# Traced durations in a planner's costs for the tails' norms, and the second chunk's front behind the first chunk's work

## The chip, the cores and the metric

The kernel runs on one core of one Trainium2 chip. The metric is the device time of one execution in microseconds. The engines and queues have short names: PE is the TensorE matmul engine (PEld its weight loads), DVE is VectorE, ACT is ScalarE, POOL is GpSimd, SP is the queue that issues most DMAs. "Filler" below means work that PE has in its queue between two steps of one chain.

## The reference

A transformer block with modulation from a condition vector, over 2048 rows of 512 columns. A is attention with 32 heads of 16 columns, B a mixer with shifted columns and an MLP of 1792 columns.

```
h = _layernorm(x) * (1 + ca) + sa
x = x + ga * _A_ref(h, A_wqkv, A_wo)          # attention, then @ wo
h = _layernorm(x) * (1 + cb) + sb
x = x + gb * _B_ref(h, B_w1, B_w2, B_w3, B_w4)
# _B_ref(x):
h = gelu(layernorm(x) @ w1)                   # then each quarter of the columns is shifted by rows: +1, -1, +2, -2
x1 = x + hs @ w2
return x1 + gelu(layernorm(x1) @ w3) @ w4
```

So each row goes through `wo`, a norm with its own scale and shift (the front's first norm), a second norm, `w1`, a gelu, the shift, `w2`, a third norm, `w3`, a gelu and `w4`.

## The kernel before

The 2048 rows are four chunks of 512 rows, and a chunk is four tiles of 128 rows (tiles 0 to 3 are chunk 0, 4 to 7 chunk 1, and so on). All matrices are split into a high and a low part, so that each product is three matmuls (L360, L362, L364). Attention takes the first 1510 us of the profiled execution; what comes behind it is called the tail here and runs to the end.

The tail of a chunk is a Python generator, `tail(ci)`, and behind it `rest(ci)`. Its steps on PE are, in order:

- **oT**: 16 transposes of the attention's output (`osb`, L1260), which ACT (L354) and DVE (L350) split into the tile `A`.
- **wo**: 12 matmuls of 512 columns for each row tile. Behind a tile's `wo` stands its norm chain: x1_add (DVE L1425), statistics (DVE L371, L372, L1367), a power on POOL (L1370), the functions `center` (DVE L1434) and `scale` (DVE L1437), statistics again, three small POOL instructions (L1370, L1374, L1375; the function `shift`), and the application on ACT (L1381), which writes the tile `xn` (chunk 0) or `xf` (chunks 1 to 3).
- **T**: 8 transposes of `xn` or `xf` for a pair of row tiles (L1260), split again into `A`. T(1,0) is the first pair of chunk 1, T(1,1) the second.
- **w1**: matmuls of 256 columns, and a gelu of six instructions over ACT, DVE and POOL (L1475 to L1479).
- **w2**: 12 matmuls of 512 columns for a row tile, xb_add (DVE L1530), the third norm (L371 to L1381), and a scaling (DVE L1534) and an addition (POOL L1535) that the output needs.
- **T4**: transposes of the third norm's `xn`.
- **w3** and **w4** in pairs of 128 columns of the MLP (`fi` counts them): w3 with a gelu, w4 onto `x1`. In chunk 0 the weights of w3 and w4 are split afresh, from the tile `raw` into `wr`: POOL L1223 for w4, ACT L1224, DVE L1225.

The order on each engine is fixed when the program is built, by a planner (`Sched`). It keeps a clock per engine in which every step advances by a written cost. `one()` walks a list of generators from the front and lets the first one whose gate is open place its next matmul on PE; `chain` queues the steps of other engines, `misc` places them when the planned clock of their engine comes near. A norm's transposes are placed on PE when the planner believes that the norm is done: the costs decide how much other PE work stands between a `wo` and its T. On the chip every engine then works through its list in order and waits on semaphores; the plan's clock is not there any more.

Costs before, in planned ns: statistics 752, the power 464, the three POOL steps 850, ACT's application 479, `center` 1355 and `scale` 602, from the helpers

```
def cA(n=CH):
    return n / 1.2 + 52
def cD(n=CH):
    return n / 0.96 + 69
```

The generators of chunks 1 to 3 are put at the front of the list, ahead of what is left of `tail(0)`. Two gates hold chunk 1: its `tail` starts when all `w1` of chunk 0 is placed, and each of its `wo` waits for the third norm of tile 2 (`("xn4", 2) in done`, since `HOLD` is 0). `x1_loads` issues the four loads of a chunk's input tiles from ACT's queue (L1317) when its `tail` starts.

Of the kernel before, what the change touches and what calls it, by code (L numbers as in the profile page):

```python
# [14 lines left out]
AF = mybir.ActivationFunctionType  # L15
# [5 lines left out]
S, D, H, DH, F = 2048, 512, 32, 16, 1792  # L21
# [21 lines left out]
XX = 170.0  # L43
# [24 lines left out]
NB = 1  # L68
# [5 lines left out]
WSPL = 1  # L74
ZPRIO = 2
NPRIO = 1
HOLD = 0
NLOW = 1
CLOW = 1150
OUTW = 7000.0  # L80
# [238 lines left out]
# [6 lines that stand above are left out]
# [7 lines left out]
def kernel(ctx, tc, A_x, A_wqkv, A_wo, B_w1, B_w2, B_w3, B_w4, c, w_mod, out):  # L332
    nc = tc.nc
    te, act, dve, pool, dma = nc.tensor, nc.scalar, nc.vector, nc.gpsimd, nc.sync
# [35 lines left out]
    def ln_stats(st, mv, src):  # L370
        dve.bn_stats(st, src)  # L371
        dve.bn_aggr(mv, st)  # L372
# [49 lines left out]
    sch = Sched()  # L422
    done = set()
# [812 lines left out]
    def pool_of(ci):  # L1236
        return fa if ci < NB or (ci - NB) % 2 else tp
# [28 lines left out]
    def spawn(gen, key):  # L1266

        def run():
            yield from gen
            done.add(key)  # L1270
        sch.add(run(), 0)
# [25 lines left out]
    def tail(ci):  # L1297
        end = ci == NC - 1
        t0 = ci * TPC
        early = ci < NB  # L1300
        if ci:
            yield lambda: ("w1", ci - 1) in done
        yield lambda: ("att", ci) in done
        new = list(range(t0, t0 + TPC))
# [40 lines left out]
        def wo_mm(i, ks):  # L1345
            if i not in banks:
                banks[i] = dbank("wo")
            A, c = As[i // 2], slice(i % 2 * P, i % 2 * P + P)
            return rows_mm(banks[i], lambda k, p: A[:, k, p, c], wo, ks, KT)
# [9 lines left out]
        def ln_ops(src, mean=False):  # L1359

            st = fa.tile([P, 6], F32, name="tst", tag="tst", bufs=8)
            mv = fa.tile([P, 2], F32, name="tmv", tag="tmv", bufs=10)
            rs = fa.tile([P, 2], F32, name="trs", tag="trs", bufs=10)

            def stats():
                ln_stats(st, mv, src)
                dve.tensor_scalar(mv[:, 1:2], mv[:, 1:2], EPS, None, op0=OP.add)  # L1367

            def rstd():
                pool.tensor_tensor(rs[:, 0:1], mv[:, 1:2], mhalf[:, 0:1], op=OP.pow)  # L1370

            def shift():
                rstd()
                pool.tensor_tensor(rs[:, 1:2], mv[:, 0:1], rs[:, 0:1], op=OP.mult)  # L1374
                pool.tensor_scalar(rs[:, 1:2], rs[:, 1:2], -1.0, 1.0, op0=OP.mult, op1=OP.mult)  # L1375
            if mean:
                return rs, mv, (("D", cD() + 150, stats), ("G", 464, rstd))
            return rs, (("D", cD() + 150, stats), ("G", 850, shift))

        def ln_apply(dst, src, rs):  # L1380
            return ("A", cA(), lambda: act.activation(dst, src, AF.Identity, bias=rs[:, 1:2], scale=rs[:, 0:1]))  # L1381

        def later(key, fn):
            yield lambda: key in done
# [4 lines left out]
        def normed(key, t, rs):  # L1389
            tag = xtag(key, t)  # L1390
            xlive[tag] = xlive.get(tag, 0) + 1
            if tag == "x4":
                x = tp.tile([P, D], F32, name="xn", tag=tag, bufs=XN[tag])
            else:
                x = xns[tag][:, xnum[tag] % XN[tag]]
                xnum[tag] += 1
            xn[key, t] = x
            y = xbt[t]
            return ln_apply(x, y, rs), mark((key, t))
# [6 lines left out]
        def xn_room(key, t):  # L1406
            return xlive.get(xtag(key, t), 0) < XN[xtag(key, t)]

        def norm_T(ts, key, i):

            yield lambda: all((key, t) in done for t in ts) and (key == "xn" or not ci or ("w3", ci - 1) in done)
            An[key, i] = A = tA("A4" if key == "xn4" else "A", i, len(ts) * P)
            yield from transposed(lambda k, j: xn[key, ts[j]][:, k * P:(k + 1) * P], range(KT), len(ts), A)
            xlive[xtag(key, ts[0])] -= len(ts)

        for i, t in enumerate(new):
            yield lambda: ci != 1 or i < HOLD or ("xn4", 2) in done
            yield lambda: sch.room() and xn_room("xn", t) and t in x1t and sch.now() >= arr.get(("x1", t), 0.0) and (ci < 2 or ("z", t - 2 * TPC) in done)
            yield from wo_mm(i, range(KT))
            b = banks.pop(i)  # L1420
            x1 = x1t[t]
            xb = xbt[t] = xbs[:, t % XBF] if pool_of(ci) is fa else tp.tile([P, D], F32, name="xb", tag="xb", bufs=XBT)

            def x1_add(x1=x1, b=b):
                dve.tensor_tensor(x1, x1, b, op=OP.add)  # L1425
                sch.free(b)

            r, m, ops = ln_ops(x1, True)
            r2, ops2 = ln_ops(xb)

            def center(xb=xb, x1=x1, m=m, ops=ops):
                ops[0][2]()
                sch.late = sch.put("G", 464, sch.T["D"] - cD() + XX, ops[1][2]) + XX
                dve.scalar_tensor_tensor(xb, x1, m[:, 0:1], cbrow, op0=OP.subtract, op1=OP.mult)  # L1434

            def scale(xb=xb, r=r):
                dve.scalar_tensor_tensor(xb, xb, r[:, 0:1], sbrow, op0=OP.mult, op1=OP.add)  # L1437

            go = partial(sch.chain, ("D", cD(), x1_add), ("D", 2 * cD() + 150, center), ("D", cD(), scale), *ops2,
                         *normed("xn", t, r2), bank=b)  # L1440
            go()
            if i % 2:
                spawn(norm_T(grp[i // 2], "xn", i // 2), ("T", ci, i // 2))
# [55 lines left out]
        for gi, ts in enumerate(grp):  # L1499
            yield lambda: ("T", ci, gi) in done  # L1500
            A = An["xn", gi]
# [19 lines left out]
        for si, ts in enumerate(sub):  # L1521
            yield lambda: all(("g", ci, i, n) in done for i in range(1 + (t0 + 1 in ts)) for n in range(4))
            for t in ts:
                yield lambda: sch.room() and xn_room("xn4", t)
                b = dbank("w2")
                yield from rows_mm(b, lambda k, p: g[:, k, p, 130 + (t - t0) * P - SH[k]:][:, :P], w, range(KT), KT)
                xb, x1 = xbt[t], x1t[t]

                def xb_add(xb=xb, b=b):
                    dve.tensor_tensor(xb, xb, b, op=OP.add)  # L1530
                    sch.free(b)

                r, ops = ln_ops(xb)
                z = (("D", cD(), lambda xb=xb: dve.scalar_tensor_tensor(xb, xb, 2.0, gbrow, op0=OP.mult, op1=OP.mult)),  # L1534
                     ("G", cG(), lambda xb=xb, x1=x1: pool.tensor_tensor(x1, x1, xb, op=OP.add)), mark(("z", t)))  # L1535
                sch.chain(("D", cD(), xb_add), *ops, *normed("xn4", t, r),
                          (None, 0, lambda z=z: sch.chain(*z, prio=ZPRIO)), bank=b, prio=NPRIO)
            spawn(norm_T(ts, "xn4", si), ("T4", ci, si))
# [88 lines left out]
    for k, blk in enumerate(blocks + [[]] * (LAG + CPER)):  # L1627
# [76 lines left out]
        if blk and blk[0] <= 2 * (NS - T0S) <= blk[-1]:  # L1704
            sch.add(tail(0))
# [9 lines left out]
    with ExitStack() as ex:  # L1715
        ep = ex.enter_context(tc.tile_pool(name="ep", bufs=1, space=PSUM))
        psd["d"], psd["s"] = ep, False
        att.close()
        akx.close()
        tpx = ExitStack()  # L1720
        tp = tpx.enter_context(tc.tile_pool(name="tp", bufs=1))
        big["A"] = tp.tile([P, 4 * KT * 2 * P], F32R, name="A")
        big["g2"] = tp.tile([P, 4 * KT * 2 * P], F32R, name="g2")
        done.add("C")
        rings["f"] = Ring(FRONT * (NC - NB), [("wf", BF)] * BF)
        for ci in range(NB, NC):
            sch.add(tail(ci), ci - NB)
        while sch.busy():
            sch.step()
        tpx.close()  # L1730
# [29 lines left out]
```

## Time and profile before

| | us |
|---|---|
| median of 3 runs (lowest, highest) | 1996.83 (1995.67, 1999.66) |
| profiled execution | 1994.44 |
| its span, first to last instruction | 1992.3 |
| PE busy in the span | 1931.4 (97%) |
| DVE, POOL, ACT busy | 1655.6, 1552.9, 1518.5 |

PE is busy nearly throughout. In the tail PE's list is long and in order, so an idle stretch of PE there is time lost; the views of the section below are read for these stretches, and for what ends each. [...]

### The profile page before, as it was taken

The numbers are of one execution on the slowest core, as the hardware profiler recorded it, in microseconds if no ns is written. First come the engines' busy times: TensorE is split into PE (matmuls) and PEld (weight loads), VectorE is DVE, ScalarE is ACT, GpSimd is POOL, SyncE is SP. The second block draws the span as 40 slices with busy tenths as digits, with TensorE's granted clock in tenths as the row PEclk, the third lists the DMA queues.
The fourth block names the chain that finished last, engine by engine and source line by source line (L and its number), as shares of the span: only waits on it lengthen the run. The fifth ranks groups of instructions, "written<-read, shape, count | busy, mean of one in ns | idle before, by whom it ended". The sixth has DMA issues, their size and how long they took to land.

```text
span 1992.3 us, 41624 instructions
## 1 busy us (share of the span) xinstructions
PE 1931.4 (97%) x14456; PEld 1155.7 (58%) x14456; DVE 1655.6 (83%) x2979; ACT 1518.5 (76%) x3100; POOL 1552.9 (78%) x1473
## 2 busy tenths in 40 slices
PE   7999999999999999999999999999998999999999
PEld 5755554554444444444444444444446888888998
DVE  6398888879999999999999999999975886656443
ACT  6438987768999999999999999999985545344333
POOL 6339998888999999999999999999995564435222
PEclk9989999999999999999999999999998999999999
DMA  8777666455434444444444444464415667553541
GB/s 303 232 193 195 163 174 173 129 134 125 97 80 101 82 99 83 99 82 100 84 98 84 98 82 99 83 161 106 97 39 197 239 247 273 208 207 120 199 148 69
DMA packets 185506, 277.99 MB, mean 140 GB/s; under 512 B 117104, under 2 KB 127856, under 8 KB 169008
## 3 DMA queue, kind: packets, MB, share of 16 engines
q1 hardware_dynamic: 181792, 267.20, 49.4%
q10 hardware_dynamic: 2304, 4.20, 0.7%
q0 software_dynamic: 1200, 3.93, 0.5%
q8 instruction: 115, 1.88, 0.4%
q14 instruction: 95, 0.78, 0.1%
HBM read 211.81 MB, written 62.91 MB: 138 GB/s over the span
## 4 chain that ended last, share of the span: by engine, by line
PE 70%; DVE 15%; ACT 5%; issue 4%; POOL 3%; DMA 2%; SPq 1%; ACTq 0%; POOLq 0%; DVEq 0%
PE mb L998 17%; PE sc L1025 11%; PE pv L1099 11%; DVE mx L994 11%; PE w L364 5%; PE w L360 5%; PE w L362 5%; PE pv L1096 5%; PE ot L1126 3%; ACT pt L1021 3%; PE xT L1260 1%; POOL trs L1370 1%; POOL pt L1074 1%; DMA wr<-Ws 1%; SPq L136 1%
## 5 line engine op out<-in xcount | busy, mean ns | idle before, releaser
L994 DVE TENSOR_REDUCE mx<-mb 128x1 f32<-128x512 f32 x2048 | 1250.9, 686 | 55.7 <-PE mb L998 48.7
L1074 POOL TENSOR_SCALAR pt<-pt 128x1024 f16<-128x1024 uint16 x773 | 1017.6, 1366 | 67.3 <-ACT pt L1021 66.9
L1021 ACT ACTIVATE pt<-sc 128x512 int32<-128x512 f32 x1688 | 890.1, 623 | 89.8 <-PE mb L998 67.5
L998 PE MATMUL mb<-kst,qtl 62*128 62x512 f32 x2048 | 786.4, 463 | 17.2 <-ACT pt L1021 7.9
L1025 PE MATMUL sc<-qtl,kst 64*128 64x512 f32 x2048 | 743.9, 450 | 3.1 <-DVE mx L994 1.8
L998 PEld LDWEIGHTS mb<-kst,qtl 62*128 62x128 f32 x2048 | 361.7, 192 | 260.7 <-ACT pt L1021 136.4
L1025 PEld LDWEIGHTS sc<-qtl,kst 64*128 64x128 f32 x2048 | 336.9, 185 | 188.4 <-DVE mx L994 119.7
L1099 PE MATMUL pv<-pt,vst 128*32 128x512 f16 x3376 | 318.0, 395 | 4.6 <-ACT ac L1116 4.6
L1479 POOL TENSOR_TENSOR g<-sq,g 128x256 fp32r<-128x256 f32 (+1 forms) x124 | 96.7, 784 | 190.0 <-ACT g L1478 177.6
L1074 POOL TENSOR_SCALAR xbs<-xbs 128x1024 f16<-128x1024 uint16 x165 | 219.4, 1362 | 4.3 <-ACT xbs L1021 4.3
L1021 ACT ACTIVATE xbs<-sc 128x512 int32<-128x512 f32 x360 | 199.8, 640 | 10.8 <-PE mb L998 9.7
L1099 PEld LDWEIGHTS <-vst 128*32 128x32 bf16 x4096 | 91.2, 94 | 182.1 <-issue 163.3
L1096 PE MATMUL pv<-pt,vst 128*32 128x512 f16 (+1 forms) x1688 | 172.5, 391 | 1.4 <-POOL pt L1074 1.3
L362 PE MATMUL w<-A,wr 128*128 128x256 f32 (+1 forms) x520 | 154.1, 296 | 0.3 <-DVE A L350 0.3
L360 PE MATMUL w<-A,wr 128*128 128x256 f32 (+1 forms) x520 | 153.9, 296 | 0.0
L364 PE MATMUL w<-A,wr 128*128 128x256 f32 (+1 forms) x520 | 153.8, 296 | 0.0
L1475 ACT ACTIVATE sq<-w 128x256 f32<-128x256 f32 (+1 forms) x130 | 52.0, 400 | 127.4 <-PE w L364 117.7
L364 PE MATMUL w<-wr,g 128*128 128x512 f32 x270 | 106.4, 394 | 3.1 <-POOL g L1479 3.1
L360 PE MATMUL w<-wr,g 128*128 128x512 f32 x270 | 106.7, 395 | 1.6 <-DMA wr<-Ws 1.6
L362 PE MATMUL w<-wr,g 128*128 128x512 f32 x270 | 106.2, 393 | 0.0
L1457 DVE SCALAR_TENSOR_TENSOR sq<-sq,w 128x256 f32<-128x256 f32 (+1 forms) x130 | 58.1, 449 | 55.4 <-ACT sq L1477 55.3
L362 PEld LDWEIGHTS w<-A,wr 128*128 128x128 f32 x520 | 99.3, 191 | 1.6 <-DVE A L350 0.5
(172 smaller groups left out, 2453.7 us busy)
## 6 DMA issues: line engine op xcount, KB each, us to landing
wr<-Ws SPq DMA_DIRECT2D x66, 1024.0 KB, 5.6
vst<-Vs SPq DMA_DIRECT2D x64, 768.0 KB, 5.1
kst<-Ks SPq DMA_DIRECT2D x126, 384.0 KB, 6.0
Ws<-wr SPq DMA_DIRECT2D x14, 1024.0 KB, 5.0
qtl<-Qs SPq DMA_DIRECT2D x128, 96.0 KB, 4.1
Vs<-vt SPq DMA_DIRECT2D x32, 384.0 KB, 4.4
Ks<-qk SPq DMA_DIRECT2D x16, 512.0 KB, 4.0
Qs<-qk SPq DMA_DIRECT2D x16, 512.0 KB, 3.0
```

Of the source, the lines that this page charges most:

```text
L360: te.matmul(o, lh, rh, start=first, stop=False)
L362: te.matmul(o, lh, rl, start=False, stop=False)
L364: te.matmul(o, ll, rh, start=False, stop=last)
L994: end = sch.crit("D", 605, e + PX, lambda: dve.reduce_max(mxs[u][:, j, g, c:c + 1], b, axis=AX.X))
L998: return ready, lambda: te.matmul(b, lhs, kst[u % 3][r, c * CH:(c + 1) * CH], start=True, stop=True), after
L1021: ea = sch.crit("A", 480, e + PX, lambda: act.activation(pt[s][:, j], b, AF.Exp))
L1025: return ready, lambda: te.matmul(b, kst[u % 3][r, kt * P:(kt + 1) * P], qst[u][r], start=True, stop=True), after
L1074: e_low[s] = XP["G"] + sch.crit("G", 1345, ready, lambda: pool.tensor_scalar(o, i, 0.5, 1.0, op0=OP.mult, op1=OP.mult))
L1096: te.matmul(acc[r:r + n, :], v[:, kt + i, c:c + n].bitcast(F16), pt[s + i].bitcast(F16)[:, j, 0::2], start=False, stop=kt == NKT - 2, skip ...
L1099: te.matmul(acc[r:r + 32, :], v[:, kt, r:r + 32], pt[s].bitcast(F16)[:, j, 1::2], start=kt == 0, stop=False, skip_group_check=True)
L1126: te.matmul(b[:, t * n:(t + 1) * n], ac[:, t * P:(t + 1) * P], smat.rearrange("p j d -> p (j d)"), start=True, stop=True)
L1479: ("G", cG(n), lambda: pool.tensor_tensor(lo, sq, hi, op=OP.subtract)), (None, 0, end), bank=b)
```

## The change

```
-HOLD = 0
...
-        if ci:
+        if ci > 1:
             yield lambda: ("w1", ci - 1) in done
...
             if mean:
-                return rs, mv, (("D", cD() + 150, stats), ("G", 464, rstd))
-            return rs, (("D", cD() + 150, stats), ("G", 850, shift))
+                return rs, mv, (("D", 1050, stats), ("G", 560, rstd))
+            return rs, (("D", 1050, stats), ("G", 1120, shift))
...
-            return ("A", cA(), lambda: act.activation(dst, src, AF.Identity, bias=rs[:, 1:2], scale=rs[:, 0:1]))
+            return ("A", 815, lambda: act.activation(dst, src, AF.Identity, bias=rs[:, 1:2], scale=rs[:, 0:1]))
...
-            yield lambda: ci != 1 or i < HOLD or ("xn4", 2) in done
...
-                sch.late = sch.put("G", 464, sch.T["D"] - cD() + XX, ops[1][2]) + XX
+                sch.late = sch.put("G", 950, sch.T["D"] - 750 + XX, ops[1][2]) + XX
...
-            go = partial(sch.chain, ("D", cD(), x1_add), ("D", 2 * cD() + 150, center), ("D", cD(), scale), *ops2,
+            go = partial(sch.chain, ("D", cD(), x1_add), ("D", 1050 + 750, center), ("D", 750, scale), *ops2,
...
         for ci in range(NB, NC):
-            sch.add(tail(ci), ci - NB)
+            sch.add(tail(ci))
```

The planner counts longer norms, `tail(1)` to `tail(3)` stand behind what is left of `tail(0)` in the list, and chunk 1 has neither of its gates. No instruction's work is changed, but 2 of the attention's last halvings of `pt` go from POOL (L1074) to ACT (L157).

The order is told at three places. Line numbers of the changed file are one to two lower there.

PE, at the end of attention, before: `xn` are the norms of tiles 2 and 3, `w1_...` the first `w1` of that pair, `osb1` chunk 1's attention output.

```order
L1260 MATMUL xT_24573<-ident_64,xn_7635 128x128 x4
L1260 MATMUL xT_24600<-ident_64,xn_7635 128x128 x4
L360 MATMUL w1_24610<-A_7633,wr_21841 128x256
...
L1260 MATMUL xT_24692<-ident_64,osb1_7627 128x128 x4
L1260 MATMUL xT_24701<-ident_64,osb1_7627 128x128 x4
L1260 MATMUL xT_24714<-ident_64,osb1_7627 128x128 x4
L1260 MATMUL xT_24719<-ident_64,osb1_7627 128x128 x4
L360 MATMUL w2_24726<-wr_24449,g1_24451 128x512
```

The same place now:

```order
L1259 MATMUL xT_24600<-ident_64,osb1_7627 128x128 x4
L1259 MATMUL xT_24606<-ident_64,osb1_7627 128x128 x4
L1259 MATMUL xT_24618<-ident_64,osb1_7627 128x128
L1259 MATMUL xT_24620<-ident_64,xn_7635 128x128 x4
L1259 MATMUL xT_24625<-ident_64,xn_7635 128x128 x4
L1259 MATMUL xT_24618<-ident_64,osb1_7627 128x128 x3
L1259 MATMUL xT_24637<-ident_64,osb1_7627 128x128 x4
L359 MATMUL w1_24646<-A_7633,wr_21841 128x256
```

All 16 oT transposes of chunk 1 now stand ahead of chunk 0's second `w1` pair, 9 of them ahead of that pair's own transposes; behind that `w1` come 15 `wo` matmuls of tiles 4 and 5, then w2 (36), then 21 more `wo` (tiles 5 and 6), and T4 behind them, with w3 right behind T4. Before, T4 followed w2 directly and 36 `wo` followed T4.

ACT at the same place, before:

```order
L1475 ACTIVATE sq<-w_24536 128x256
L1477 ACTIVATE sq<-sq 128x256
L1475 ACTIVATE sq<-w_24551 128x256
L354 ACTIVATE A<-xT 128x2x256
L1477 ACTIVATE sq<-sq 128x256
L1478 ACTIVATE g_24451<-sq 128x256
L354 ACTIVATE A<-xT 128x2x256
```

And now:

```order
L1473 ACTIVATE sq<-w_24549 128x256
L1476 ACTIVATE g_24451<-sq 128x256
L1475 ACTIVATE sq<-sq 128x256
L1316 DMA x_24592<-in_A_x_dram 128x512
L1316 DMA x_24594<-in_A_x_dram 128x512
L1316 DMA x_24596<-in_A_x_dram 128x512
L1316 DMA x_24598<-in_A_x_dram 128x512
L353 ACTIVATE A<-xT 128x2x256
L1476 ACTIVATE g_24451<-sq 128x256
L353 ACTIVATE A<-xT 128x2x256
L1380 ACTIVATE xn<-xbs,trs 128x512
L353 ACTIVATE A<-xT 128x2x256 x4
```

Tile 3's application (L1380) stood ahead of these rows before, and now stands behind the four DMA issues and two copies of `A`.

DVE between the last w2 of chunk 0 and T4's split, before (`xbs` rows are third norms, the last L1530 is tile 2's):

```order
L1530 TENSOR_TENSOR xbs<-xbs,w_24770 128x512
L371 BN_STATS tst<-xbs 128x6
L372 BN_AGGR tmv<-tst 128x2
L1367 TENSOR_SCALAR tmv<-tmv 128x1
L1534 SCALAR_TENSOR_TENSOR xbs<-xbs,gbrow 128x512
L1225 TENSOR_TENSOR wr<-raw,wr 128x512 x4
L1534 SCALAR_TENSOR_TENSOR xbs<-xbs,gbrow 128x512
L350 TENSOR_TENSOR A<-xT,A 128x384 x4
```

And now:

```order
L1528 TENSOR_TENSOR xbs<-xbs,w_24800 128x512
L1224 TENSOR_TENSOR wr<-raw,wr 128x512
L1532 SCALAR_TENSOR_TENSOR xbs<-xbs,gbrow 128x512
L1224 TENSOR_TENSOR wr<-raw,wr 128x512 x3
L370 BN_STATS tst<-xbs 128x6
L371 BN_AGGR tmv<-tst 128x2
L1366 TENSOR_SCALAR tmv<-tmv 128x1
L1423 TENSOR_TENSOR x_24594<-x_24594,wo 128x512
```

Tile 2's statistics now stand behind four splits of fresh weights and one L1532; between them and T4's first split (L349) come two x1_add, two L1532, one more split and `center` of tile 5.

## Rows read from the trace of the kernel before

**Rows 1.** Stretches: start:end, length, busy PE, PEld, DVE, ACT, POOL, PEclk, DMA, GB/s.

```profile
1510.60:1523.62 13.02, 10.52 (x74) 9.90 (x73) 5.41 (x12) 5.89 (x15) 3.54 (x6) 0.87 0.66 246
1523.62:1549.51 25.89, 21.07 (x88) 16.91 (x87) 20.63 (x40) 10.48 (x20) 11.35 (x16) 0.87 0.61 212
1549.51:1582.00 32.49, 28.92 (x172) 26.68 (x171) 29.14 (x57) 19.55 (x41) 22.59 (x30) 1.00 0.60 215
1660.00:1992.30 332.30, 323.33 (x1951) 290.65 (x1949) 175.70 (x365) 134.49 (x327) 118.91 (x178) 1.00 0.45 164
```

**Rows 2.** Waits of PE from 1500 us on: waiter, releaser, total us, times, longest.

```profile
PE xT L1260 <- ACT xf L1381: 8.6, 6, 2.0
PE xT L1260 <- ACT xn L1381: 4.8, 3, 2.9
PE w L364 <- POOL g L1479: 3.1, 2, 2.2
PE xT L1260 <- DVE sq L1457: 2.2, 1, 2.2
```

**Rows 3.** PE in order of time: start, us, instruction, [idle before, releaser].

```profile
1510.60 0.60 PE L1260 MATMUL xT<-ident,xn 128*128 128x128 f32 x4
1513.36 0.66 PE L1260 MATMUL xT<-ident,xn 128*128 128x128 f32 x4 [2.16 <-DVE sq L1457]
1516.20 0.41 PE L362 MATMUL w<-A,wr 128*128 128x256 f32 x1
1516.42 0.41 PE L364 MATMUL w<-A,wr 128*128 128x256 f32 x1
1519.20 0.28 PE L362 MATMUL w<-A,wr 128*128 128x256 f32 x1
1519.32 0.28 PE L364 MATMUL w<-A,wr 128*128 128x256 f32 x1
1523.62 0.48 PE L360 MATMUL w<-wr,g 128*128 128x512 f32 x1
1531.90 0.39 PE L364 MATMUL w<-wr,g 128*128 128x512 f32 x1
1537.77 2.40 PE L1260 MATMUL xT<-ident,xn 128*128 128x128 f32 x10 [2.94 <-ACT xn L1381]
1549.51 0.33 PE L360 MATMUL w<-A,wr 128*128 128x384 f32 x1
1554.01 0.34 PE L364 MATMUL w<-A,wr 128*128 128x384 f32 x1
1555.98 0.98 PE L1260 MATMUL xT<-ident,xf 128*128 128x128 f32 x7 [1.52 <-ACT xf L1381]
```

**Rows 4.** ACT (ACTq: its DMA issues) and DVE near the end of attention.

```profile
1511.67 0.59 ACT L354 ACTIVATE A<-xT 128x512 fp32r<-128x512 f32 x1
1512.64 0.40 ACT L1478 ACTIVATE g<-sq 128x256 fp32r<-128x256 f32 x1
1521.94 2.39 ACTq L1317 DMA_DIRECT2D x<-in_A_x_dram  x4
1512.90 0.41 DVE L1457 SCALAR_TENSOR_TENSOR sq<-sq,w 128x256 f32<-128x256 f32 x1
```

**Rows 5.** DVE, POOL and ACT between the last w2 of chunk 0 and T4.

```profile
1533.19 0.68 DVE L1530 TENSOR_TENSOR xbs<-xbs,w 128x512 f32<-128x512 f32 x1
1535.52 3.58 DVE L1225 TENSOR_TENSOR wr<-raw,wr 128x512 fp32r<-128x512 f32 x4
1535.09 0.93 POOL L1370 TENSOR_TENSOR trs<-tmv,mhalf 128x1 f32<-128x1 f32 x1 [0.26 <-DVE tmv L1367]
1536.90 0.81 ACT L1381 ACTIVATE xn<-xbs,trs 128x512 f32<-128x512 f32 x1 [0.38 <-POOL trs L1375]
```

**Rows 6.** POOL in order of time, in front of a w4 of chunk 0.

```profile
1623.54 0.99 POOL L1370 TENSOR_TENSOR trs<-tmv,mhalf 128x1 f32<-128x1 f32 x1 [6.38 <-DVE tmv L1367]
1624.50 1.01 POOL L1479 TENSOR_TENSOR g<-sq,g 128x384 fp32r<-128x384 f32 x1
```

**Rows 7.** PE in order of time, at the end of attention.

```profile
1496.89 0.40 PE L1096 MATMUL pv<-pt,vst 128*32 128x512 f16 x3 [0.72 <-POOL pt L1074]
```

## The prediction, made before the changed kernel was run

> **What bounds the kernel now.** I read the stretches of the tail first, then PE's waits, then PE in order of time at each wait, then the engine that ended it. In the tail PE is the bound: from 1660 us on it is busy 323.3 of 332.3 us [rows 1]. No matmul is added or taken away, so the change is worth what it does to PE's idle time and to the TensorE clock. From 1500 us on four kinds of wait make up 18.7 us [rows 2]: 8.6 for `xf`, six times (the second norm of chunks 1 to 3 was not done when PE came to its transposes); 4.8 for `xn` (nearly all at T4, 1532.6 to 1537.8); 3.1 for POOL's `g`; 2.2 for a bank at the end of attention. Two of the stretches also run at a mean clock of 0.87 [rows 1]. In the first, `w1` starts every 0.22 us instead of 0.12 for 16 matmuls [rows 3]: 1.6 us. In the second, ten transposes take 2.40 us where seven take 0.98 at full clock [rows 3], about 1.0 us more, and about six `wo` behind them cost some 0.2 more each: 2.2 us.
>
> **Waits for `xf`: taken away.** A norm's transposes stand where the planner thinks it done, so longer costs put more PE work between a `wo` and its T. I counted the matmuls between the second tile's last `wo` and T in both orders. They go at 0.12 us (256 columns), 0.17 (384: 1549.51 to 1554.01 is 26 starts) and 0.24 (512: 1523.62 to 1531.90 is 35) [rows 3]. The distances before and now are: T(1,0) 7.5 and 11.8; T(1,1) 13 and 19; T(2,0) 14 and 22; T(2,1) 10 and 17; T(3,0) 7.5 and 14; T(3,1) 7 and 16 us. Each grows by 4 to 9 us, and the longest wait was 2.0 [rows 2]. I take five as gone; T(1,0) I leave at its 1.52, because DVE comes to its norm late (below). That is 8.6 - 1.5 = **-7.1 us** (bounds -8.6 and -4). What hides these norms now is w1, w3 and w4 of other chunks.
>
> **The end of attention: dearer.** Before, four transposes at 1510.60 ran in a free bank, and PE then waited until 1513.36 for the bank that DVE's gelu step at 1512.90 released [rows 3, 4]. Now the first `osb` transposes are in that bank (the order names both `xT_24600`): PE waits 2.76 us instead of 2.16. Nine transposes later, at about 1514.3, it needs tile 3's `xn`. On ACT that now stands behind four DMA issues, two copies of `A` and a `g`. The issues took 2.39 us together where they stood before [rows 4]; from about 1512.8 they end at 1515.2. Then 0.59 + 0.40 + 0.59 [rows 4] and 0.81 for the application [rows 5] make 1517.6 (1516.4 if the issues pass faster). Fifteen transposes (1.8 us) and 48 `w1` (5.8) bring 1525.2 at full clock. Before, the same work ended at 1523.62, with 1.6 us of slow clock in it. PE is idle for nearly 6 us here, twice 2.8 to 3, so I expect at least as much slow clock: 1.6 us as now, at most 4.8 (all 48 `w1` at 0.10 more). The result is +1.8 to +6.5; I take **+3.0**, nearer to the lower end, since 1.6 us is what the one case seen at this place cost.
>
> [...]
>
> **Around T4: even.** Before, T4 had nothing in front of it: from the end of w2 (1532.1) to its third norm (1537.77) is 5.6 us. Now 21 `wo` stand there, 5.0 us of cover. But DVE has four splits of weights ahead of tile 2's statistics, 3.58 us [rows 5], and the chain becomes 8.3 to 9.2 us; PE waits about 3.5 instead of 4.8: -1.3. What is late next is T4's split. Between these statistics and the split, DVE has four instructions of 0.68, a split of 0.9 and a `center` with its statistics (about 1.8): 5.4 us. POOL, ACT and the first transposes take 3.6 of it (from the end of the statistics at about 1535.0 to 1537.77, and a copy) [rows 3 to 5]. `wo` covered this before; w3 follows at once now, so PE waits about 2.4 (1 to 3). The slow clock of the stretch should cost some 1 us less, since part of it falls into this wait. Sum **0** (-3 to +3). Behind it DVE still has tile 6's `center` ahead of tile 5's second statistics, therefore the 1.52 at T(1,0) stays.
>
> [...]
>
> **Other terms.** A w4 waited 2.2 us for a `g` that stood on POOL behind a power, and POOL had waited 6.38 us for DVE's statistics [rows 2, 6]. With 950 for the power and 1050 for the statistics the plan puts later `g` nearer to where POOL is; I take half, **-1.1** (0 to -2.2). Chunk 0's w3 and w4 now come earlier against chunk 1's w1, on weights that DVE must have split: **+1.0** (0 to +5) for new waits. Two halvings move from POOL, for which PE waited 0.72 [rows 7], to ACT: **-0.4** (-0.7 to +0.7). The early loads cost SP nothing: they go from ACT's queue, which is counted above. The other gate (`("w1", 0)`) only lets oT forward.
>
> **Sum.** +3.0 + 0 - 7.1 - 1.1 + 1.0 - 0.4 = -4.6 us. The profiled execution, 1994.44, becomes 1989.8; it stands 2.4 under the median, so the median goes from 1996.83 to **1992.2**, or -0.23%. About 0.2% (4 us) is what a measurement of this kernel can tell from no change; the forecast lies just outside.
>
> **The rivals.**
> *The front eats it.* The clock stays low through all 48 `w1` (+3 over my term) and DVE comes late to T4's split (+1): -4.6 + 4 = -0.6, so 1996.2. For it: two stretches with idle PE and 0.87 today [rows 1]. Against it: the slow clock cost only 1.6 us there today, behind a wait of 2.16.
> *Slower: DVE becomes the bound between T(1,0) and w2 of chunk 1.* From 1549.5 to 1582 DVE is busy 29.1 of 32.5 us already [rows 1]. The change brings one more pair of w3 and w4 into that place: four splits at 0.9 [rows 5] and their gelu and additions, some 8 us of DVE against 8.4 us of PE, so DVE's 3.4 us of slack is needed for the norms that fell behind at T4. If it falls short by 4.5 us or more, PE waits that long, and norms behind it are late again (1.5 and 2.0 at T(2,0) and T(2,1) return): -4.6 + 4.5 + 3.5 + 1 = +4.4, so 2001.2. It decides where w3 waits for `wr` from DVE; before there is no such wait [rows 2].
> *The plan doesn't do what it says* would need the T's not to move; the order shows that they do.
>
> **How the numbers follow.** The forecast has 0.5, with its own range 1987 to 1994; the front eating it 0.33; slower 0.17. About a tenth is left out on each side. 1987.0 is where the waits for `xf` and `g` go wholly (-1.5 and -1.1 more), no new ones come (-1.0) and the front is at its lower end (-1.2): -9.4. 1999.5 leaves out the upper half of the slower rival. The forecast's range reaches a little into "same" and the second rival's best end into "faster": faster 0.5, same 0.33, slower 0.17.
>
> **What would show it.** Right: no wait of PE for `xf` behind T(1,0); a wait for `xn` of about 3 us in the 24 transposes at 1514; T4's wait near 3.5 and a wait for DVE's `A` behind it. Wrong: waits for `xf` that remain (DVE is later than the costs say), a wait of w3 for DVE's `wr`, or a clock of 0.5 far beyond 1522 us.

## The result, and the profile after

The change makes the kernel slower: median 2003.62 us (14 runs, 1998.45 to 2006.77) against 1995.70 for the kernel before (14 runs), ratio 1.003 with a 95% interval of 1.002 to 1.0041. The forecast was 1992.2. The profiled execution of the changed kernel took 2006.77 us (span 2004.8), 3.2 us above its median; before it was 1994.44 (span 1992.3), 1.3 below. Line numbers of the changed kernel are one to two lower: L1259 are the transposes, L359 to L363 the matmuls, L1380 ACT's application, L1224 DVE's split of fresh weights.

Waits of PE from 1500 us on, in the profile of the changed kernel (waiter, releaser, total us, times, longest):

```profile
PE w L359 <- DMA wr<-Ws: 10.0, 3, 5.9
PE xT L1259 <- ACT xn L1380: 5.5, 2, 3.3
PE w L363 <- POOL g L1477: 3.3, 2, 2.4
PE xT L1259 <- ACT xf L1380: 3.2, 3, 1.5
PE w L361 <- DVE A L349: 2.2, 1, 2.2
PE xT L1259 <- DVE sq L1455: 1.8, 1, 1.8
```

The waits for `xf` fell from 8.6 us in six [rows 2] to 3.2 in three. The first line is the new one, and nothing in the prediction has a term for it: PE waits 10.0 us for weights that are loaded from memory (`Ws`). Before, the same line stood in this view too, with three waits:

```profile
PE w L360 <- DMA wr<-Ws: 1.6, 3, 0.8
```

PE in order of time in the changed kernel, at its waits (start, us, instruction, [idle before, releaser]):

```profile
1513.25 0.99 PE L1259 MATMUL xT<-ident,osb 128*128 128x128 f32 x7 [1.83 <-DVE sq L1455]
1516.81 0.90 PE L1259 MATMUL xT<-ident,xn 128*128 128x128 f32 x3 [2.24 <-ACT xn L1380]
1546.57 1.31 PE L1259 MATMUL xT<-ident,xn 128*128 128x128 f32 x10 [3.26 <-ACT xn L1380]
1550.24 0.69 PE L361 MATMUL w<-A,wr 128*128 128x384 f32 x1 [2.18 <-DVE A L349]
1551.05 0.52 PE L359 MATMUL w<-A,wr 128*128 128x384 f32 x1
1586.48 0.98 PE L1259 MATMUL xT<-ident,xf 128*128 128x128 f32 x7 [0.84 <-ACT xf L1380]
1603.06 0.79 PE L359 MATMUL w<-wr,g 128*128 128x512 f32 x1 [5.87 <-DMA wr<-Ws]
1604.07 0.63 PE L363 MATMUL w<-wr,g 128*128 128x512 f32 x1
1707.82 0.50 PE L359 MATMUL w<-wr,g 128*128 128x512 f32 x1 [3.35 <-DMA wr<-Ws]
```

The waits at 1603.06 and 1707.82 stand in front of the seventh `w2` matmul of chunks 1 and 2. The stretches that answer to [rows 1], and those around the two long waits for weights (columns as there; PEclk is the share of full speed that the TensorE clock was granted, 1.0 or 0.5 in every record of both traces, with a mean over the span of 0.993 before and 0.988 after):

```profile
1511.42:1526.26 14.84, 10.77 (x72) 10.53 (x73) 7.38 (x14) 8.63 (x19) 2.83 (x7) 0.77 0.65 247
1526.26:1550.24 23.98, 18.54 (x87) 14.87 (x86) 20.35 (x40) 9.21 (x18) 12.82 (x21) 0.97 0.56 204
1550.24:1560.21 9.97, 9.97 (x43) 9.75 (x44) 9.62 (x19) 4.45 (x9) 4.52 (x7) 0.74 0.42 146
1599.00:1607.00 8.00, 3.94 (x10) 3.12 (x11) 1.05 (x3) 0.42 (x1) 0.68 (x2) 0.57 0.87 335
1707.50:1713.00 5.50, 5.18 (x16) 4.12 (x17) 1.72 (x4) 0.25 (x1) 0.93 (x3) 0.69 0.23 98
```

**Where the 12.5 us between the two profiled spans lie.** I took each matmul of the tail at a fixed interval (0.231, 0.173, 0.117 and 0.123 us for 512, 384, 256 columns and a transpose; the medians from start to start in the tail of before are 0.230, 0.174, 0.120 and 0.109): the 2688 matmuls are 449.2 us in both kernels (449.5 by the medians). What is left is idle time, slow clock and restarts (the first matmul behind the wait at 1707.82 had the next 0.34 us behind it at a granted clock of 1.0, the two after it 0.23).

| us | before | after |
|---|---|---|
| end of attention (0.12 us after the start of the last w1 matmul ahead of the first transpose of this place) | 1510.6 | 1511.3 |
| from there to the end of the last matmul | 478.0 | 488.3 |
| of it the waits (before: the 18.7 of [rows 2], 1.6 for `wr` and 0.3 for `A`) | 20.6 | 26.1 |
| of it the rest: slower clock, restarts after waits | 8.2 | 13.0 |
| from the last matmul to the end of the span | 3.7 | 5.3 |

So 5.5 us are waits (+8.4 for loads, -5.4 for `xf`, the rest +2.4), 4.8 are clock and restarts, 1.6 lie behind the last matmul, and 0.7 come from attention, whose end moves by more than that from one profile to the next (1508.8 to 1517.6 in those of this study). The parts are rounded. These two executions lie further apart than the kernels do: the medians differ by 7.9 us, and a ratio of 1.003 is 6 us. A second profile of the changed kernel (e10_after_again, 2001.24 us), counted in the same way against before, has +3.7 for waits, +3.2 for clock and restarts, +1.8 behind the last matmul and -1.8 from attention.

**What PE waits for at 1603.06.** The class `Ring` deals out homes in SBUF to pieces of weights of 1 MB, and issues a load as soon as a home is handed back. A chunk's `wo`, `w1` and `w2` are two pieces each, and share three homes: two of their own and that of chunk 1's `osb`. So the first `w2` piece comes into a home of `wo`, and the second into that of the first `w1` piece. That one is read until the last group of `w1` is half done. Behind it PE has 24 `w1` matmuls (2.8 us) and the first six of `w2`, which use the first piece (1.4 us). This is 4.2 us of cover for a load of 1 MB, in both kernels (4.2 to 4.4 in all three chunks). The planner counts such a piece as there when its load is issued.

The chain of work that ended last has the second `w2` pieces of chunks 1, 2 and 3 in it (start of the load, us to its landing). Before:

```profile
1585.65 5.00 DMA wr<-Ws
1687.67 4.82 DMA wr<-Ws
1812.65 4.82 DMA wr<-Ws
```

After:

```profile
1593.71 9.30 DMA wr<-Ws
1700.25 7.53 DMA wr<-Ws
1836.62 4.99 DMA wr<-Ws
```

The wait is the landing less what is left of the cover. Before: 5.0 - 4.2 = 0.8, and 0.4 twice. After, 9.30 less the 3.5 us from the issue at 1593.71 to the end of PE's work at 1597.2 is 5.8. SP's own queue around it, in the changed kernel (start, us, transfer):

```profile
1588.13 0.33 SPq L135 DMA_DIRECT2D Ws<-wr  x1
1588.51 5.16 SPq L135 DMA_DIRECT2D raw<-in_B_w_dram  x2
1593.71 1.13 SPq L135 DMA_DIRECT2D wr<-Ws  x1
1595.38 0.33 SPq L135 DMA_DIRECT2D Ws<-wr  x1
1595.81 0.36 SPq L135 DMA_DIRECT2D raw<-in_B_w_dram  x1
```

PE was done with the home at 1592.9, and SP came to the load at 1593.7, behind a raw load that had waited for its buffer: 0.8 us late. Of the 5.1 us by which this wait is longer than before, the other 4.3 are the landing itself (9.30 against 5.00). Stores of chunk 0's freshly split weights (`Ws<-wr`, 1 MB) stand before and behind the load; the one before had landed by 1593.5, and the one behind was issued 1.7 us after the load. In chunk 2 there are no stores; two loads of `w4` and `w3` stand right ahead of the piece at 1700.25:

```profile
1695.77 0.32 SPq L135 DMA_DIRECT2D wr<-Ws  x1
1697.15 0.32 SPq L135 DMA_DIRECT2D wr<-Ws  x1
1700.25 0.32 SPq L135 DMA_DIRECT2D wr<-Ws  x1
```

Before, in the order of SP, two other loads stand between the two `w2` pieces of chunk 2, now four. The later `T`'s push the last group of `w1` behind one more pair of `w3` and `w4`, and so the load behind theirs.

The three loads of before took 4.8 to 5.0 us to landing, which is already more than the cover of 4.2 to 4.4 us.

### The profile page after: what moved, and what is told of

Read it like the earlier page. It is cut to its first block, busy times and chain, and to the rows that moved or that the text cites. A ratio compares the mean times of both kernels' runs of the same rounds, so it can differ in the third digit from the quotient of the medians.

```text
span 2004.8 us, 41630 instructions
## 1 busy us (share of the span) xinstructions
PE 1937.5 (97%) x14456; PEld 1160.5 (58%) x14456; DVE 1659.9 (83%) x2979; ACT 1524.9 (76%) x3102; POOL 1549.6 (77%) x1471
## 4 chain that ended last, share of the span: by engine, by line
PE 74%; DVE 13%; ACT 4%; issue 3%; DMA 3%; POOL 2%; SPq 0%; ACTq 0%; DVEq 0%; POOLq 0%
PE mb L997 17%; PE sc L1024 12%; PE pv L1098 11%; DVE mx L993 10%; PE w L359 6%; PE w L363 6%; PE w L361 6%; PE pv L1095 5%; PE ot L1125 3%; ACT pt L1020 2%; DMA wr<-Ws 1%; PE xT L1259 1%; POOL pt L1073 1%; PE q L363 1%; PE v L359 1%
## 5 line engine op out<-in xcount | busy, mean ns | idle before, releaser
L359 PE MATMUL w<-A,wr 128*128 128x256 f32 (+1 forms) x520 | 154.5, 297 | 0.0
L363 PE MATMUL w<-A,wr 128*128 128x256 f32 (+1 forms) x520 | 154.0, 297 | 0.0
L359 PE MATMUL w<-wr,g 128*128 128x512 f32 x270 | 108.8, 403 | 10.0 <-DMA wr<-Ws 10.0
L363 PE MATMUL w<-wr,g 128*128 128x512 f32 x270 | 108.9, 403 | 3.3 <-POOL g L1477 3.3
L361 PE MATMUL w<-wr,g 128*128 128x512 f32 x270 | 107.9, 400 | 0.0
L156 ACT ACTIVATE pt<-pt 128x1024 f16<-128x1024 uint16 x73 | 102.0, 1398 | 0.0
```

The costliest lines, as they stand in the source:

```text
L156: fn()
L359: te.matmul(o, lh, rh, start=first, stop=False)
L361: te.matmul(o, lh, rl, start=False, stop=False)
L363: te.matmul(o, ll, rh, start=False, stop=last)
```

## The experiments

**Theory L** (late loads): the loss is PE's wait for the second `w2` pieces and the slow clock behind it. **Rival F** (the front): the loss comes from the new order between 1511 and 1560 us.

**e1_costs and e2_order: one half of the change at a time.** e1_costs has all the longer costs of the change and not the order (against the kernel before, in part):

```
-            return rs, (("D", cD() + 150, stats), ("G", 850, shift))
+            return rs, (("D", 1050, stats), ("G", 1120, shift))
...
-            go = partial(sch.chain, ("D", cD(), x1_add), ("D", 2 * cD() + 150, center), ("D", cD(), scale), *ops2,
+            go = partial(sch.chain, ("D", cD(), x1_add), ("D", 1050 + 750, center), ("D", 750, scale), *ops2,
```

> The order and the gates of before, with the longer costs of the changed kernel's norms alone. Theory L (late loads): what the changed kernel lost is PE's wait for the second w2 piece of a chunk, 10.0 us against 1.6, since that piece has only 4.2 us of PE work as cover and lands late when other transfers stand next to it. In this order chunk 2's piece has two other loads right ahead of it on SP, as in the changed kernel, so a wait of about 3.3 us stays there; chunk 1's has a store right ahead and 5.1 us of cover, a wait of 1 to 5. The waits for xf fall from 8.6 to about 2.5. Sum against before: -6 for xf, +3 to +7 for the loads, about +2 of slow clock behind them: ratio 0.9995 to 1.0015. Rival F (the front): the loss comes from the new order between 1511 and 1560 us, which is not in this kernel: 5 us faster than before, ratio 0.997 to 0.998.

e2_order has the order and not the costs:

```
-        if ci:
+        if ci > 1:
...
-            yield lambda: ci != 1 or i < HOLD or ("xn4", 2) in done
...
-            sch.add(tail(ci), ci - NB)
+            sch.add(tail(ci))
```

> The list order without gates of the changed kernel, with the norm costs of before. Theory L: chunk 1's second w2 piece has a store, raw loads and 4.2 us of cover, so PE waits 3 to 6 us for it; those of chunks 2 and 3 have the neighbours that they had before (two loads, not four), so 0.4 each. The waits for xf stay near 8. Sum against before: +3 to +5 for the load, +2 of slow clock, and the front within 1 of even: +5 to +8, ratio 1.0025 to 1.004. Rival F: the same sign but through the front; then PE's waits for wr stay under 2 us in all and the time between the end of attention and the first w3 grows by 4 us or more.

Measured: the costs alone 1.0056 (1.0041 to 1.0071), the order alone 1.0029 (1.0018 to 1.0039), both slower, and the costs alone slower than both together. The costs alone fall outside what either theory had. Their waits for weights are 8.1 us, as theory L has it, but T4's wait grew as well, from 2.94 [rows 3]:

```profile
1541.50 2.40 PE L1260 MATMUL xT<-ident,xn 128*128 128x128 f32 x10 [6.82 <-ACT xn L1381]
1611.44 0.50 PE L360 MATMUL w<-wr,g 128*128 128x512 f32 x1 [3.41 <-DMA wr<-Ws]
```

With the order alone the load of chunk 1 costs 1.92 us and not the 3 to 6 that were expected; its largest wait is that of T(1,0) for its norm, where the short costs leave too little filler:

```profile
1560.48 1.76 PE L1259 MATMUL xT<-ident,xf 128*128 128x128 f32 x7 [7.62 <-ACT xf L1380]
1591.15 0.50 PE L359 MATMUL w<-wr,g 128*128 128x512 f32 x1 [1.92 <-DMA wr<-Ws]
```

So neither theory carries the halves: each half has a wait at the front that the other half takes away (T4's 6.8 us needs the `wo` in front of it, T(1,0)'s 7.6 us the longer costs). Together they have neither.

**e3_land: the planner is told when the front's weights land.** Against the changed kernel:

```
+LAND = 8000.0
...
                     sch.dma(dma.dma_start, w.bitcast(F32), Ws[i])
-                    done.add(key)
+                    if self is rings.get("f"):
+                        sch.after(sch.T["P"] + LAND, partial(done.add, key))
+                    else:
+                        done.add(key)
...
-            yield lambda: ("w1", ci - 1) in done
+            yield lambda: ("w2", ci - 1) in done
```

(The last hunk keeps the next chunk from taking the pieces for which `w2` now waits.) The planner then places a pair of `w3` and `w4` of the chunk before between `w1` and `w2`: 9.4 us of cover.

> The changed kernel, with one thing more: the planner counts a front piece as there only 8 us after its load is issued, and so puts w3 and w4 pairs of the chunk before between w1 and w2 (cover of the second w2 piece 9.4 us instead of 4.2 in all three chunks). Theory L: the waits for wr fall from 10.0 to under 2 us and the slow clock behind them goes, -9 to -12 against the changed kernel: ratio to before 0.997 to 1.0. Rival F: the waits for wr go but the same idle time turns up elsewhere (w3 for the third norm, w4 for g): ratio 1.002 to 1.004 as now.

Measured: 1989.17 us, ratio 0.9965 (0.9953 to 0.9977). It is faster than both kernels, and by the two ratios some 13 us faster than the changed one (9 to 12 were expected), with the work of the instructions as it was. Its longest waits from 1500 us on:

```profile
PE xT L1263 <- ACT xn L1384: 5.6, 2, 4.3
PE w L360 <- DVE x L1581: 2.0, 1, 2.0
PE xT L1263 <- ACT xf L1384: 1.9, 2, 1.2
```

The rest are 4.6 us (for a bank, `g` and `A`). No wait for `wr` is left, and the idle time did not turn up elsewhere: 14.1 us against 26.0. Theory L holds, and rival F falls, since the front is the same here: when PE has done 40 us of the 449.2 us of work, it has lost 13.9 us to waits, clock and restarts before, 14.7 in the changed kernel and 15.2 with the delay. Between 60 and 80 us of work, where chunk 1's `w2` lies, it loses 0.9, 7.7 and 0.1.

**e8_land5: a shorter delay.** The same with `LAND = 4500.0`, which makes the cover 5.8 to 6.0 us.

> e3_land with a delay of 4.5 us in place of 8, so that the cover of the second w2 pieces is 5.8 to 6.0 us, between the 4.2 of the changed kernel and the 9.4 of e3_land. Theory L, in which PE waits for the landing time less the cover: with landings of 8 to 9.3 us in chunk 1, 6.5 to 7.5 in chunk 2 and 5 to 6.5 in chunk 3 the waits are 2.5 to 4, 1 to 2 and 0 to 1, 3.5 to 7 in all, and the time lies between the two: 1992 to 1998, ratio 0.998 to 1.001. Rival (the gain of e3_land comes from the other order of w3 and w4 and not from cover): a time like that of e3_land or like that of the changed kernel, with no such step in the waits.

Measured: ratio 0.9976 (0.9964 to 0.9988), a little under the range that was expected, 1992.92 us. The waits are 2.76 and 1.43 us, 4.2 in all, and none in chunk 3:

```profile
1601.44 0.50 PE L360 MATMUL w<-wr,g 128*128 128x512 f32 x1 [2.76 <-DMA wr<-Ws]
1699.29 0.51 PE L360 MATMUL w<-wr,g 128*128 128x512 f32 x1 [1.43 <-DMA wr<-Ws]
```

4.2, 5.9 and 9.4 us of cover give 10.0, 4.2 and 0 us of waits: they go with the cover.

**e4_nostore: are the stores what makes chunk 1's piece late?** The changed kernel without its 14 stores of split weights; the later chunks load other pieces of the same size instead, so their `w3` and `w4` products are of other weights.

```
-                    sch.dma(dma.dma_start, w.bitcast(F32), Ws[i])
+                    sch.dma(dma.dma_start, w.bitcast(F32), Ws[i if i in FRONT else FRONT[i % len(FRONT)]])
...
-                sch.dma(dma.dma_start, Ws[i], w.bitcast(F32))
+                sch.dma(lambda o, x: None, Ws[i], w.bitcast(F32))
```

> The changed kernel without the 14 stores of chunk 0's freshly split w3 and w4 (chunks 1 to 3 load other pieces of the same size in their place, so these do not multiply by the right weights). It asks whether the 1 MB stores next to chunk 1's second w2 piece make it land late. Theory L with stores as the cause: the piece lands in 5 to 6 us instead of 9.3 and PE's wait at w2 of chunk 1 falls from 5.9 to 0.5 to 2; chunk 2's wait of 3.4 stays, since its neighbours are loads. If the raw loads or the row of small packets are the cause, the wait at chunk 1 stays over 4.

Measured (one execution, 1997.59 us): the same loads in the chain of work that ended last, and PE at chunk 1's `w2`.

```profile
1590.53 5.22 DMA wr<-Ws
1691.35 6.51 DMA wr<-Ws
1826.70 6.16 DMA wr<-Ws
```

```profile
1595.80 0.50 PE L359 MATMUL w<-wr,g 128*128 128x512 f32 x1 [1.82 <-DMA wr<-Ws]
```

With the stores away chunk 1's piece lands in 5.2 us instead of 9.3 and the wait falls from 5.87 to 1.82, although the raw loads are still there. In chunk 2, with the two loads ahead, the landing is 6.5 us and the wait 2.33; in the two profiles of the changed kernel they are 7.5 and 7.1, and 3.35 and 2.90. Chunk 3's landing is 6.2 us (5.0 and 5.6 there). So the stores make chunk 1's piece late, as far as one execution without them tells. Why it is that late stays open: in e2_order a raw load 0.4 us ahead and a store, a raw load and a load 1.8 to 2.9 us behind go with 6.1 us, and in the changed kernel almost the same ones with 8.2 and 9.3.

**e6_traffic: a store put behind the loads of the kernel before.** Right behind the load of each second `w2` piece SP issues a store of 1 MB to a place that nothing reads.

```
                     sch.dma(dma.dma_start, w.bitcast(F32), Ws[i])
+                    if i == order["w2"][1] and self is rings.get("f"):
+                        dma.dma_start(spare, self.last.bitcast(F32))
+                    self.last = w
```

> The kernel before with three transfers more: right behind the load of the second w2 piece of chunks 1, 2 and 3 a store of 1 MB to a place in memory that nothing reads. It asks whether a store that is issued after a load slows the load. Theory L (transfers next to each other share the engines): the three loads land in 6.5 to 9 us instead of 4.8 to 5.0, PE waits 1.6 to 4 us more for each, ratio 1.003 to 1.006. Rival (first come, first served): landing times and waits as before, ratio within 0.001.

Measured: ratio 1.0027 (1.0015 to 1.0039), a little under the range that was expected. The waits for `wr`, and two of the loads in the chain (that of chunk 1 is not in it):

```profile
PE w L360 <- DMA wr<-Ws: 6.6, 3, 2.3
```

```profile
1693.78 6.67 DMA wr<-Ws
1820.62 6.48 DMA wr<-Ws
```

The store that was issued 0.4 us after the load made it land 1.7 to 1.9 us later (1.4 in chunk 1), and PE waited 6.6 us instead of 1.6. This alone made the kernel before as slow as the changed one. Here a store that followed a load counted, then, and not only what stood ahead of it. A load that followed did not: in the kernel before the load of chunk 3 has another of 1 MB 0.37 us behind it, and landed in 4.82 us.

**e5_before_land, e7_costs_land, e7b_order_land: the delay without the change, and with each half of it.** The same `LAND` lines in the kernel before, in e1_costs and in e2_order (in the last hunk the gate of chunk 1, where there is one, stays).

> The kernel before, with the delay of e3_land alone (a front piece counts as there 8 us after its load is issued; cover of the second w2 pieces 9.3 us). It asks how much of e3_land's 6.3 us against before comes from the delay and how much from the change. Theory L: before had only 1.6 us of waits for these loads, so 1 to 3 us are to be had: ratio 0.9985 to 0.9995, and the change itself is worth some 4 to 5 us once the loads are covered, as the sum without the loads said (-4.6). Rival: the delay sorts the tail better by itself, whatever the loads do: ratio 0.9965 here too, and the change is worth nothing.

> The longer norm costs alone, with the delay of e3_land. Theory L: the 8.1 us of waits for wr of e1_costs go and a little slow clock with them, -9 to -11 against e1_costs: 1996 to 1998.5, ratio 1.0 to 1.0015; the wait of T4 for xn (6.8 us) and that for xf (4.4) stay, so that this comes out worse than e3_land by their difference. Rival (e1_costs lost by something other than the loads): ratio over 1.003.

> The list order without gates alone, with the delay of e3_land. Theory L: only 3.7 us of waits for wr are to be had here: -3 to -5 against e2_order, 1996.5 to 1998.5, ratio 1.0005 to 1.0015; the waits for xf (14.3 us, 7.6 in one at T(1,0)) stay, since the norms' costs are the short ones. Rival: ratio under 0.999, then the order alone carries e3_land's gain.

Measured, each against the kernel before on the same chip:

| ratio (95% interval) | as it is | with the delay |
|---|---|---|
| kernel before | 1 | 0.9990 (0.9981 to 0.9999) |
| costs alone | 1.0056 (1.0041 to 1.0071) | 1.0008 (0.9998 to 1.0017) |
| order alone | 1.0029 (1.0018 to 1.0039) | 1.0019 (1.0011 to 1.0027) |
| both (the change) | 1.0030 (1.0020 to 1.0041) | 0.9965 (0.9953 to 0.9977) |

The delay is worth 2 us where the loads cost 1.6 us of waits, and 10 and 13 us where they cost 8.1 and 10.0; the order alone, with 3.7 us, gains 2, less than expected. So it does not sort the tail better by itself. With the loads covered the change is worth 0.9965 / 0.9990, or 5 us (2 to 8 with the two intervals). Against the kernel before with the same delay each half is a loss even then: 1.0008 / 0.9990 is 1.0018, and 1.0019 / 0.9990 is 1.0029.

**e10_after_again: the changed kernel once more.**

> The changed kernel once more, for a second profile of it. If the late landings belong to its order, the second w2 pieces of chunks 1 and 2 again land in over 8 and over 6.5 us and the waits for wr are again 8 to 11 us. If they were an accident of one execution, they fall under 4 us here. It also asks whether the last store, 3.5 us to landing in the first profile against 2.0 in the kernel before, is slow again.

Measured (one execution, 2001.24 us): the waits, and the loads in the chain.

```profile
PE w L359 <- DMA wr<-Ws: 9.2, 3, 4.8
```

```profile
1590.77 8.23 DMA wr<-Ws
1696.40 7.09 DMA wr<-Ws
```

The late landings belong to the order of the transfers and not to one execution. The last store was slow again, too (3.6 us to landing; below).

## Why the prediction was wrong

**The step that failed** is the one on new waits: "Chunk 0's w3 and w4 now come earlier against chunk 1's w1, on weights that DVE must have split: +1.0". It looked for them on DVE alone, and no wait for DVE's `wr` came. Of SP the text says only that "the early loads cost SP nothing". A moved `w3` takes its raw loads and its 1 MB store with it, and a moved `T` pushes the last `w1` group and the load that waits for it: neither was followed in SP's order, and the loads had no price. They cost +8.4 us of waits, and some 3.3 of the +4.8 of clock and restarts: behind the waits at 1603.06 and 1707.82 eight matmuls each start 0.43 us apart instead of 0.23, with a mean granted clock of 0.57 and 0.69 in these stretches. The trace of before had the warning. The waits for `DMA wr<-Ws` were the row that I left out of [rows 2]: three, one in each chunk at the same place, of 0.4 to 0.8 us. Such a wait says that this load has no slack, so that what delays it is paid in full, as the 0.8 us of later issue and the 4.3 us of longer landing were in chunk 1. The rivals missed it as well: the slower one had the right sign and the right size (2001.2), but its mechanism (DVE short of time between T(1,0) and `w2`, seen in `w3` waiting for `wr`) did not come.

**The other steps, term by term**, in the profiled execution:

- Waits for `xf`: -5.4, predicted -7.1. T(1,0), the one that I had left, has no wait; T(1,1), T(2,0) and a later one keep 0.84, 1.53 and 0.86.
- End of attention: +2.0, predicted +3.0 and at least +1.8. From the end of the last `w1` ahead of this place it took 14.84 us; before, 12.86 (that `w1` started at 1510.48 and took 0.28; the row of [rows 1] begins at 1510.60). The path was the one that was worked out: the four DMA issues on ACT ended at 1514.56, the application ran to 1516.75, and PE went on at 1516.81 (worked out: 1516.4 to 1517.6). Slow clock and restarts cost 0.5 more than before (2.4 us against 1.9 beside the waits).
- T4: even, as predicted, by parts that partly differ. Its wait was 3.26 (3.5), the new one for DVE's `A` 2.18 (2.4). Of the 6.9 us of slow clock (1548.6 to 1555.5) only 1.6 fell into that wait, however: the stretch up to the end of the wait for `A` is 2.1 us shorter (23.98 against 25.89, with one `w3` of 0.17 in it), and then 16 `w3` start 0.32 us apart instead of 0.17 (2.4 us), at a granted clock of 0.74 against 1.0 from the first `w3` on before [rows 1].
- POOL's `g`: +1.8, predicted -1.1. It is the same wait in front of a `w4`, at 1640.97 now, 2.42 us where it was 2.23; but seven matmuls behind it start 0.43 us apart now, and none did before, which is 1.6 of the +4.8.
- The halvings: not to be told, since attention's end moves by several us between executions (1508.8 to 1517.6).

Without the loads these are -1.3 us for a predicted -4.2 (all terms but the halvings), and the comparison with the loads covered gives -5 (-2 to -8). For `xf`, the end of attention and T4 the mechanism was read rightly, the gain at `g` did not come, and what was missing was a resource that the change loads. Of the prediction's own signs of being wrong two came: waits for `xf` that remained, and a clock of 0.5 far beyond 1522 us (from 1548.6 to 1555.5, 1599.8 to 1606.7, 1640.8 to 1644.2 and 1709.1 to 1712.5; before, from 1536.0 to 1542.8). One figure of its text needs a word: the sum of its lower end, -9.4, gives 1987.4 and not 1987.0.

**Not predicted by anything:** 1.6 us behind the last matmul (last section).

## What to carry to other kernels

Where a planner or a list moves work on one engine, follow the transfers that move with it, and give each load a price: time to landing, less the work between the release of its buffer and its first use (here 4.8 to 9.3 us, less 4.2). The wait of 0.4 to 0.8 us that returned at the same place in every chunk was a load without slack, and the planner, which counted a load as there when it was issued, put work where it made that load late (10.0 us of waits for 1.6). With the loads covered, costs and order were each a loss alone (ratio 1.0018 and 1.0029) and a gain together (0.9965 / 0.9990), so test the halves before one is kept or dropped.

## What the hardware did that I had not expected

- The same load of 1 MB landed in 4.7 to 4.8 us in chunks 2 and 3 of the kernel before and of e2_order, in 6.4 to 6.7 with a store of 1 MB issued 0.4 us behind it, in 6.5 to 7.5 with two loads of 1 MB 3 to 4.5 us ahead, in 5.0 to 6.5 with one load 4.4 us ahead (chunk 3 of four profiles, so that the same neighbours give times 1.5 us apart), and in 8.1 to 9.3 between stores and raw loads (chunk 1 of four profiles; 5.0 in the kernel before and 6.1 in e2_order, where a store was issued 2.1 and 1.8 us behind).
- Between two loads of 1 MB the one issued second was the late one. In the kernel before, from 1705 us on, seven pairs of loads of 1 MB were issued 1.4 us apart with no other large transfer in flight ahead of them: the first landed in 4.7 to 5.0 us, the second in 6.8 to 7.3. So a load ahead delayed the one behind it, as with the two loads above (6.5 to 7.5 us), and not the other way round; a store behind did delay the load ahead (6.4 to 6.7 us in e6_traffic).
- The last store of the kernel landed in 2.0 us in eight profiles and in 3.5 to 3.7 in four (the changed kernel twice, e1_costs, e4_nostore). In these four, and only there, a transfer of instructions lies in the last stretch. The DMA view of the last 4.7 us of the changed kernel (a queue with its packets, MB and share; a transfer with its size in KB and the us to landing):

```profile
q8 instruction: 1, 0.02, 1.2%
...
out_dram<-x SPq DMA_DIRECT2D x1, 256.0 KB, 3.5
```

And before, where no line of instructions stands:

```profile
out_dram<-x SPq DMA_DIRECT2D x1, 256.0 KB, 2.0
```

This goes with the 1.6 us between the two kernels behind the last matmul. That the one causes the other was not tried.
